# Halving the requests of attention's loads, and storing x from SyncE's queue instead of GpSimd's

## The chip, the cores and the metric

One Trainium2 chip, of which the program uses one core. The metric is the device time of one execution in microseconds (us), a median over runs. TensorE multiplies matrices, VectorE, ScalarE and GpSimd work on elements, SyncE issues DMAs and waits. All DMAs of the core, whichever engine issues them, are carried by the same 16 DMA engines.

## The reference

Two blocks in a row, all in float32. The first is causal sliding-window attention over 8 sequences of 576 rows, with 8 heads of 64 and a window of 64 keys. The second is a mixture of 8 experts, in which a row's expert is either its own best one or, where a local gate says so, that of the row before it.

```python
rel = pos[:, None] - pos[None, :]
mask = (rel >= 0) & (rel < window)
scores = np.where(mask, scale * np.matmul(q, k.transpose(0, 1, 3, 2)), -1e9)
attn = softmax(scores)                       # over keys
x = np.matmul(attn, v)                       # then (B, S, H*D): 4608 rows of 512

logits = x @ w_gate                          # 8 experts
local_gate = sigmoid(x @ w_local)
for b in range(B):
    for s in range(S):
        fresh_e = argmax(logits[b, s])
        e = fresh_e if s == 0 or local_gate[b, s] < 0.5 else prev_e
        prev_e = e
        h = np.maximum(x[b, s] @ w1[e], 0.0)           # 512 -> 1024
        out[b, s] = softmax(logits[b, s])[e] * (h @ w2[e])   # 1024 -> 512
```

## The kernel before

**Stages.** The 4608 rows are worked on in 9 groups of 512 (`sc` is 0 to 8). Attention takes each group in four units, one for each pair of heads (`hp` is 0 to 3), so it has 36 units. A unit is: `scores` (L385, 36 matmuls into two PSUM tiles `sp`), the exponential on ScalarE (L416) into a tile `p`, a mask on VectorE (L421) or a bias that TensorE adds beforehand, `values` (L431, 32 small matmuls into `xo`), and on VectorE the reciprocal of the row sums (L436) and the division that writes the unit's part of `x` (L441). Scores run two units ahead of values. When a group's four units are done its tile `x` (128 partitions by 4 chunks by 512 numbers, 1 MB) is stored to the DRAM tensor `xs`. Expert blocks then gather rows of `xs` by index (L1148), multiply them with `w1` and `w2` of their expert and scatter the result (L1361). The second stage starts when TensorE has done the last `values`, at about 134 us of 645.

**What attention loads.** For each group: `kq`, the keys and queries of the four head pairs (2 MB, into one tile `w` of a ring of four that the weights of the experts use later); `va`, the values with a column of ones (1 to 1.2 MB, three buffers), from which GpSimd (L361, L365) and ScalarE (L360, L363, L367) make a copy `vb` shifted by 64 rows; and, for groups 4 to 8, `vtt`, the values turned (1 MB, one buffer), from which TensorE computes the gates (`gates`, L317). The function `load` issues them on SyncE's queue, two groups ahead: `va` and the first half of `kq` after the first unit of group `sc` in program order, the second half of `kq` and `vtt` after its third. Attention's orders on TensorE, ScalarE and SyncE are written out by hand; VectorE and GpSimd are ordered by a scheduler.

**What SyncE waits for.** It executes its list in order, so a wait holds all that stands behind it. `va` of group `sc + 2` waits until TensorE has done the values of group `sc - 1`, whose buffer it takes. `vtt` waits for the gates of the group before. `until` (L239) is a DMA of four bytes that waits for an early or a late result, to hold the loads behind it back. Every DMA on the queue also takes one of eight completion semaphores in turn, and waits for the DMA that had it last. After attention's loads the queue carries the first experts' weights in 512 KB pieces (L1167), and `held` (L1471), a DMA of four bytes that waits for the first gathers, ahead of the weights of blocks 1 and 2.

**Where x is stored.** GpSimd issues one DMA for each group (L533), in its own order among the copies L361 and L365. The rows of `xs` are 528 numbers long, of which 512 are x, so that one row of one chunk is one run of 2 KB. `x` has two buffers: the first division of group `sc + 2` waits for the store of group `sc`. The first gathers wait for the stores of groups 0 to 3.

Of the kernel before, what the change touches and what calls it, by code (L numbers as in the profile page):

```python
# [19 lines left out]
P = 128  # L20
B, H, S, DH = 8, 8, 576, 64
D = H * DH
# [38 lines left out]
SC = 4 * P  # L61
# [7 lines left out]
GATED = range(4, NSC)  # L69
# [8 lines left out]
def row_of(t):  # L78

    return t + (t >= ZR)  # L80
# [87 lines left out]
def attention(ctx, tc, ring, kq, v3, v4, vt, vh, xs, lt, ok, wg, wg2, ident, rt, ex):  # L168
# [14 lines left out]
    nc = tc.nc  # L183
# [22 lines left out]
    kqs, qts, kts, vts, vas, vbs = {}, {}, {}, {}, {}, {}  # L206
# [4 lines left out]
    def space(name, sc):  # L211
        return kp.tile([P, 4, H, width(sc)], F32, name=name, bufs=2 if name == "vb" else 3)
# [6 lines left out]
    def load(sc, parts):  # L219
        for part in parts:  # L220
            if part == "turned":
                vts[sc] = tp.tile([P, HP, SC], F32, name="vtt")
                nc.sync.dma_start(out=vts[sc], in_=vt[GATED.index(sc)])
            elif isinstance(part, tuple):
                if sc not in vas:
                    vas[sc] = space("va", sc)
                src, h = v4[GATED.index(sc)] if sc in GATED else v3[sc], slice(*part)
                nc.sync.dma_start(out=vas[sc][:, :, h], in_=src[:, :, h])
            else:
                if sc not in kqs:  # L230
                    kqs[sc] = ring.tile([P, HP, 2, SC], F32, name="w")
                    kts[sc], qts[sc] = kqs[sc][:, :, 0], kqs[sc][:, :, 1]
                nc.sync.dma_start(out=kqs[sc][:, part], in_=kq[sc, :, part])

    late = cp.tile([1, 4], F32, name="late")

    def until(i, x):

        nc.sync.dma_start(out=late[:, i:i + 1], in_=x)  # L239

    pairs = slice(0, HP // 2), slice(HP // 2, HP)
    whole = (0, H)
    load(0, [slice(0, 1), slice(1, 2), (0, H // 2), pairs[1], (H // 2, H)])

    def warm(n):
# [39 lines left out]
    def build_bias():  # L285
        colf = columns()
        for c in range(2):
            for par in range(2):
                nc.vector.tensor_scalar(bias[:, c, :, par, :], colf[:, :KB // 2], rowf, LOW,
                                        Alu.is_lt if par == c else Alu.is_ge, Alu.mult)  # L290
        nc.vector.tensor_scalar(unit, colf[:, 0], rowf, None, Alu.is_equal)
        nc.vector.memset(never, LOW)
# [4 lines left out]
    def turn(sc, x, half):  # L297

        r = pair()
        for i in range(2):  # L300
            for c in range(4):
                nc.tensor.transpose(r[:, i, c * P:(c + 1) * P],
                                    x[:, c, 2 * half + i].rearrange("p j d -> p (j d)"), ident)
        o = pp.tile([P, 2, SC], F32, name="p")
        nc.scalar.copy(o, r)
        vts.setdefault(sc, []).append(o)
# [14 lines left out]
    def gates_ahead():  # L321

        r = bank()
        for hp in range(HP):
            nc.tensor.matmul(r[hp * GW:(hp + 1) * GW, :WIN], lhsT=wg2[:, hp, :], rhs=vhs[:, hp, :],
                             start=True, stop=True)
        nc.scalar.copy(ahead, r[:, :WIN])
# [7 lines left out]
    def logits(sc, gated):  # L335

        gt = back(gated).rearrange("p (c h g) -> p c g h", c=4, h=HP)[:, :, :E + 1]
        nc.vector.tensor_reduce(lt[:, 4 * sc:4 * sc + 4, :], gt, axis=AX.X, op=Alu.add)

    def spread(sc, gated):  # L340

        gt = back(gated).rearrange("p (c h g) -> p c h g", c=4, h=H)[:, :, :, :E + 1]
        g = slice(VX, VW)
        if sc == GATED[0]:
            nc.gpsimd.tensor_copy(vbs[sc][WIN:, 0, :, g], ahead_t[WIN:])
        nc.scalar.copy(vbs[sc][:WIN, :, :, g], gt[:WIN])
        nc.scalar.copy(vbs[sc][WIN:, 1:, :, g], gt[WIN:, :3])
        nc.scalar.copy(vas[sc][:, :, :, g], gt)

    def back_ahead():  # L350
        o = bank()[:WIN, :P]
        nc.tensor.transpose(o, ahead, ident)
        nc.scalar.copy(ahead_t[WIN:], o.rearrange("p (h g) -> p h g", h=H)[:, :, :E + 1])

    def shift(sc):

        va = vas[sc]
        vb = vbs[sc] = space("vb", sc)
        w = slice(width(sc - 1))
        nc.scalar.copy(vb[WIN:, 0, :, w], vas[sc - 1][WIN:, 3])  # L360
        nc.gpsimd.tensor_copy(vb[:WIN, :2], va[:WIN, :2])  # L361
        yield
        nc.scalar.copy(vb[WIN:, 1:3], va[WIN:, :2])  # L363
        yield
        nc.gpsimd.tensor_copy(vb[:WIN, 2:], va[:WIN, 2:])  # L365
        yield
        nc.scalar.copy(vb[WIN:, 3], va[WIN:, 2])  # L367

    def shift_first(half):

        va, h = vas[0], slice(4 * half, 4 * half + 4)
        if not half:
            vbs[0] = space("vb", 0)
            nc.gpsimd.memset(vbs[0][WIN:, 0], 0.0)
        nc.gpsimd.tensor_copy(vbs[0][:WIN, :, h], va[:WIN, :, h])
        nc.scalar.copy(vbs[0][WIN:, 1:, h], va[WIN:, :3, h])
# [82 lines left out]
    def step(free=True):  # L459
        nonlocal pause, side, trip  # L460
        pause -= HALF

        if side and pause <= 0.0 and (free or not trip):
            w, trip = next(side, (0.0, None))
            pause = max(pause, -HALF) + w
            if trip is None:
                side = ()
                if ex.jobs:
                    ex.rows(ex.jobs[0], -1)

    for i, (sc, hp) in enumerate(units):
        if hp == 0:
            x, g = wk.tile([P, 4, HP, 2, DH], F32, name="x"), None
            if sc in GATED:
                g = wk.tile([P, 4, HP, 2, E + 1], F32, name="g")

        if 1 < i < len(units) - LEAD:
            ps[units[i + LEAD]] = scores(*units[i + LEAD])
        if hp == (0 if sc else 3) and sc + 1 < NSC:
            moves = shift(sc + 1)  # L480
        for _ in range(2 if sc else 4):
            next(moves, None) if moves else None

        if hp == 3 and sc + 1 in GATED:
            spread(sc + 1, gated)
        elif (sc, hp) == (1, 3):
            gates_ahead()
        elif (sc, hp) == (2, 3):
            back_ahead()
        if hp == 3 and sc not in GATED:  # L490
            turn(sc, x, 0)
            old = x
        elif sc and sc - 1 not in GATED:
            if hp == 0:
                turn(sc - 1, old, 1)
            elif hp == 2:
                logits(sc - 1, turned)

        if side is None and 4 * sc >= C1 and hp >= 2:
            side = rt.first(bank)  # L500
        step(not (hp == 3 and sc + 1 in GATED))
        values(sc, hp, ps.pop((sc, hp)), x, g)
        if i < 2:
            ps[units[i + LEAD]] = scores(*units[i + LEAD])
        if i == 0:
            shift_first(1)
            until(1, allr[:1, 0, 0, 0, :1])
            load(2, [pairs[0], whole, pairs[1]])
            nc.sync.dma_start(out=vhs, in_=vh)
        if i == 2 * HP:  # L510
            with tc.issue_after(masked[-1].ins):
                rt.prepare()
                build_bias()
        if hp == 1 and sc and sc - 1 not in GATED:
            turned = gates(sc - 1)
        if hp == 2 and sc + 1 in GATED:
            gated = gates(sc + 1)
        if 0 < sc < NSC - 2 and hp in (0, 2):
            load(sc + 2, [pairs[1]] if hp else [whole, pairs[0]])
        if hp == 2 and sc + 2 in GATED:  # L520
            load(sc + 2, ["turned"])
        if (sc, hp) == (NSC - 3, 3):
            ex.jobs = [ex.weights({}, -1, ("w1",), lambda: until(2, allr[:1, sc, hp, 0, :1]))]
            if side == ():
                ex.rows(ex.jobs[0], -1)
        step(not (hp == 2 and sc + 1 in GATED))
        if (sc, hp) == (NSC - 2, 1):
            ex.weights(ex.jobs[0], -1, ("w2",), lambda: until(3, allr[:1, sc, hp, 0, :1]))
        if hp == HP - 1:
            if sc in GATED:  # L530
                nc.vector.tensor_reduce(lt[:, 4 * sc:4 * sc + 4, :], g.rearrange("p c h j e -> p c e (h j)"),
                                        axis=AX.X, op=Alu.add)
            nc.gpsimd.dma_start(out=xs[row_of(sc * SC):row_of(sc * SC) + SC, :D].rearrange("(c p) d -> p c d", p=P),  # L533
                                in_=x.rearrange("p c h j d -> p c (h j d)"))
    while side:
        step()

# [1030 lines left out]
```

## Time and profile before

| | |
|---|---|
| median of 3 runs (lowest, highest) | 646.91 us (645.65, 647.38) |
| the profiled execution | 646.97 us |
| its span, first to last instruction | 645.2 us |
| granted TensorE clock, mean | 0.997 |
| TensorE busy with matmuls in the span | 619.5 us (96%) |
| attention, 5 to 135 us | TensorE busy 116.0 of 130 us, DMA share 0.96, 363 GB/s |
| experts, 135 to 645.2 us | TensorE busy 501.1 of 510.2 us, DMA share 0.64, 231 GB/s |
| stores of x (L533), GpSimd | 9 of 1024 KB, 0.76 us each to issue |
| loads of kq | 17 of 1024 KB and 2 of 512 KB, issue to landing 10.2 us (median) |

The busy time of TensorE is modelled at the ends of its instructions, so its share says where it was supplied with work and not that it ran at its peak. The DMA share is the mean over the 16 DMA engines; it can come out a little over 1 in a short stretch, since a packet's time includes what it waited for on its way. "Idle before" in the timelines and waits is the time an engine stood still ahead of an instruction, with the event that ended it; "issue" means that the profile shows no event that it waited for.

### The profile page before, as it was taken

Reading aid. Unit: us, or ns where it says so; the run is one execution under the profiler, and the core shown is the slowest. Engines: PE = TensorE matmul, PEld = TensorE weight load, DVE = VectorE, ACT = ScalarE, POOL = GpSimd, SP = SyncE. Lnnn points to the kernel's source line nnn. Section 1 sums busy time; section 2 is a strip of 40 time slices with the busy share of each in tenths; the row PEclk is TensorE's granted clock in tenths of the full one; section 3 lists DMA queues with packets and bytes.
Section 4 is the critical chain, followed back from the end, with each engine's and each line's share of the span. In section 5 each row is a group of like instructions: output and inputs, shape, how many; then the busy total and the mean of one; then the engine's idle time right before and its main releaser. Section 6 shows DMA issues by size and latency. Waiting matters only on the chain. (4 is left out here: it accounts for less than half of the span.)

```text
span 645.2 us, 14856 instructions
## 1 busy us (share of the span) xinstructions
PE 619.5 (96%) x6319; PEld 535.8 (83%) x6319; DVE 386.7 (60%) x730; ACT 199.9 (31%) x364; POOL 130.0 (20%) x132
## 2 busy tenths in 40 slices
PE   8889998899999999999999999999999999999995
PEld 7777776785859999978998999887997998899995
DVE  6676588853874865273553683362917752876730
ACT  4766665611473122112120312021211221122120
POOL 5322112320003202111212220221312022101101
PEclk9999999999999999999999999999999999999998
DMA  8999999969736655686957655769768557945501
GB/s 331 416 349 344 379 359 368 344 241 356 210 146 233 242 199 197 209 314 244 398 193 274 229 226 217 259 232 366 258 244 302 186 196 255 354 157 221 216 17 38
DMA packets 29318, 166.43 MB, mean 258 GB/s; under 512 B 8451, under 2 KB 9497, under 8 KB 20026
## 3 DMA queue, kind: packets, MB, share of 16 engines
q1 hardware_dynamic: 20394, 135.54, 57.8%
q0 software_dynamic: 8848, 29.85, 11.9%
q8 instruction: 52, 0.85, 0.5%
q14 instruction: 24, 0.20, 0.1%
HBM read 146.18 MB, written 19.59 MB: 257 GB/s over the span
## 5 line engine op out<-in xcount | busy, mean ns | idle before, releaser
L1361 POOL DMA_INDIRECT out_dram<-y,idx x36 | 41.3, 1148 | 347.3 <-DVE y L1297 169.6
L1240 PE MATMUL hp<-xs,ws 128*128 128x128 f32 x672 | 79.6, 275 | 0.0
L1288 PE MATMUL hp<-ws,hs 128*128 128x256 f32 x336 | 77.6, 380 | 0.0
L1240 PEld LDWEIGHTS hp<-xs,ws 128*128 128x128 f32 x672 | 77.3, 192 | 0.0
L1288 PEld LDWEIGHTS hp<-ws,hs 128*128 128x128 f32 x336 | 63.5, 190 | 9.3 <-issue 0.8
L1379 PE MATMUL hp<-xt,w 128*64 128x64 f32 (+2 forms) x640 | 66.3, 276 | 1.0 <-issue 1.0
L1379 PEld LDWEIGHTS hp<-xt,w 128*128 128x128 f32 (+1 forms) x640 | 61.2, 170 | 5.9 <-issue 2.5
L1297 DVE SCALAR_TENSOR_TENSOR y<-hp,xg,kept 128x256 f32<-128x256 f32 x42 | 19.7, 481 | 71.4 <-issue 47.0
L1251 DVE TENSOR_TENSOR h<-hp,keep 128x512 f32<-128x512 f32 x42 | 28.6, 690 | 53.0 <-PE hp L1240 53.0
L1148 POOL DMA_INDIRECT xg<-xs,gx x40 | 48.2, 1205 | 44.3 <-issue 37.6
L1411 PE MATMUL yp<-w,h 128*128 128x512 f32 x128 | 56.6, 593 | 0.0
L1240 PEld LDWEIGHTS hp<-xt,w 128*128 128x128 f32 x448 | 53.2, 192 | 2.7 <-issue 1.3
L1240 PE MATMUL hp<-xt,w 128*128 128x128 f32 x448 | 54.7, 275 | 0.0
L1288 PE MATMUL hp<-w,h 128*128 128x256 f32 x224 | 53.6, 382 | 0.0
L431 PE MATMUL xo<-vb,p 128*64 128x74 f32 (+1 forms) x576 | 44.2, 228 | 6.8 <-issue 3.7
L416 ACT ACTIVATE p<-sp 128x512 f32<-128x512 f32 x72 | 39.2, 596 | 37.1 <-PE sp L385 33.9
L385 PEld LDWEIGHTS sp<-w 64*64 64x64 f32 x1296 | 37.9, 134 | 13.1 <-issue 9.7
L421 DVE TENSOR_TENSOR p<-p,mask 128x1024 f32<-128x1024 f32 x29 | 36.5, 1258 | 19.2 <-ACT p L416 18.9
L431 PEld LDWEIGHTS xo<-vb,p 128*64 128x64 f32 x576 | 38.4, 137 | 10.0 <-issue 5.2
L385 PE MATMUL sp<-w 64*64 64x128 f32 (+1 forms) x1296 | 43.3, 265 | 3.3 <-issue 2.4
L1288 PEld LDWEIGHTS hp<-w,h 128*128 128x128 f32 x224 | 41.3, 190 | 5.6 <-issue 0.4
L431 PE MATMUL xo<-va,p 128*64 128x74 f32 (+1 forms) x576 | 44.5, 228 | 1.5 <-issue 1.5
(280 smaller groups left out, 934.0 us busy)
## 6 DMA issues: line engine op xcount, KB each, us to landing
w<-in_w_dram SPq DMA_DIRECT2D x42, 2048.0 KB, 8.7
w<-in_kq_dram SPq DMA_DIRECT2D x17, 1024.0 KB, 10.2
w<-in_w_dram SPq DMA_DIRECT2D x24, 512.0 KB, 10.0
xs<-x POOLq DMA_DIRECT2D x9, 1024.0 KB
va<-in_v_dram SPq DMA_DIRECT2D x5, 1184.0 KB
vtt<-in_vt_dram SPq DMA_DIRECT2D x5, 1024.0 KB
va<-in_v_dram SPq DMA_DIRECT2D x3, 1040.0 KB, 10.2
va<-in_v_dram SPq DMA_DIRECT2D x2, 520.0 KB, 7.0
```

What stands on the lines that cost most here:

```text
L385: nc.tensor.matmul(sp[j][c * WIN:(c + 1) * WIN, a:b], lhsT=kt[h, hp, block * WIN:(block + 1) * WIN], rhs=qt[h, hp, a:b], start=not biased, ...
L416: nc.scalar.activation(p[:, j], sp[j], Act.Exp, scale=DH ** -0.5)
L421: masked.append(nc.vector.tensor_tensor(p, p, m.to_broadcast([P, 2, SC]), op=Alu.mult))
L431: nc.tensor.matmul(xo[par * WIN:(par + 1) * WIN, j, s * VW:s * VW + n], lhsT=p[:, j, b * WIN:(b + 1) * WIN], rhs=w[:, s, 2 * hp + j, :n], ...
L1148: self.nc.gpsimd.indirect_dma_start(out=x, out_offset=None, in_=self.xs[:rows, :], in_offset=bass.IndirectOffsetOnAxis(ap=gx[:, s:s + 1], ...
L1240: nc.tensor.matmul(out[:, m, :], lhsT=a[:, kk, m * P:(m + 1) * P], rhs=b[:, kk, :], start=start and m + kk == 0, stop=stop and (m, kk) == ...
L1251: nc.vector.tensor_tensor(o, x, y, op=add)
L1288: nc.tensor.matmul(out, lhsT=a[:, m, :], rhs=b[:, m, :], start=start and m == 0, stop=stop and m == FK // 2 - 1, skip_group_check=True)
L1297: nc.vector.scalar_tensor_tensor(y[i][:, j * w:(j + 1) * w], x, pw[i], y2, Alu.mult, Alu.add)
L1361: self.nc.gpsimd.indirect_dma_start(out=self.out[:, :], out_offset=bass.IndirectOffsetOnAxis(ap=st["idx"][:, s:s + 1], axis=0), in_=y, in_ ...
L1379: nc.tensor.matmul(hp[a, i, :], lhsT=st["w1"][:, kk, m * P:(m + 1) * P][:, a], rhs=st["xt"][:, kk, :n], start=(kk == 0), stop=(kk == DK - 1))
L1411: nc.tensor.matmul(yp, lhsT=st["h"][:, m, i * P:(i + 1) * P], rhs=st["w2"][:, m, :], start=(m == 0), stop=(m == FK - 1))
```

## The change

Attention's loads are requested in halves, and x is stored by SyncE:

- `vtt`: two DMAs of two head pairs each (512 KB) instead of one of 1 MB.
- `va`: where all eight heads were loaded at once, two DMAs of two chunks of 128 rows each (520 or 592 KB). The two half loads of group 0, four heads each, stay as they are.
- `kq`: one DMA for each head pair (512 KB) instead of one for two.
- `x`: two DMAs of 256 rows each (512 KB) on SyncE's queue, instead of one of 512 rows on GpSimd's. They stand at the same place of the program, after the last unit of the group, which is a place in SyncE's written order now: behind all loads issued in that group and ahead of those of the next.

```diff
             if part == "turned":
                 vts[sc] = tp.tile([P, HP, SC], F32, name="vtt")
-                nc.sync.dma_start(out=vts[sc], in_=vt[GATED.index(sc)])
+                for h in pairs:
+                    nc.sync.dma_start(out=vts[sc][:, h], in_=vt[GATED.index(sc), :, h])
             elif isinstance(part, tuple):
...
-                nc.sync.dma_start(out=vas[sc][:, :, h], in_=src[:, :, h])
+                for c in (slice(0, 2), slice(2, 4)) if h.stop - h.start == H else (slice(0, 4),):
+                    nc.sync.dma_start(out=vas[sc][:, c, h], in_=src[:, c, h])
             else:
...
-                nc.sync.dma_start(out=kqs[sc][:, part], in_=kq[sc, :, part])
+                for hp in range(part.start, part.stop):
+                    nc.sync.dma_start(out=kqs[sc][:, hp], in_=kq[sc, :, hp])
...
-            nc.gpsimd.dma_start(out=xs[row_of(sc * SC):row_of(sc * SC) + SC, :D].rearrange("(c p) d -> p c d", p=P),
-                                in_=x.rearrange("p c h j d -> p c (h j d)"))
+            for c in range(0, SC, SC // 2):
+                a = row_of(sc * SC) + c
+                nc.sync.dma_start(out=xs[a:a + SC // 2, :D].rearrange("(c p) d -> p c d", p=P),
+                                  in_=x[:, c // P:(c + SC // 2) // P].rearrange("p c h j d -> p c (h j d)"))
```

`pairs` is the two halves of the four head pairs, `HP` is 4, `H` 8, `P` 128 and `SC` 512. The order of matmuls on TensorE is the same in both kernels; 26 more of them carry a wait, because the halves have a semaphore each.

## The prediction

> **What bounds the kernel.** I read the page first, then the stages.
>
> ```profile
> span 645.2 us, 14856 instructions
> PE 619.5 (96%) x6319; PEld 535.8 (83%) x6319; DVE 386.7 (60%) x730; ACT 199.9 (31%) x364; POOL 130.0 (20%) x132
> ...
> PE   8889998899999999999999999999999999999995
> ...
> q8 instruction: 52, 0.85, 0.5%
> ```
>
> TensorE (PE) is the bound at 96%, and apart from the tail its digits fall under 9 only in the first eight slices, which are attention. The last line is the engines' own fetch of instructions: 52 packets of 16 KB, against TensorE's 12,812 records, one packet for some 250. The table of stages says how full the DMA engines are meanwhile:
>
> ```profile
> 5.00:135.00 130.00, 116.00 (x2735) 95.67 (x2735) 96.70 (x239) 79.50 (x135) 34.06 (x41) 1.00 0.96 363
> 135.00:645.20 510.20, 501.09 (x3576) 437.68 (x3574) 289.48 (x490) 119.07 (x228) 91.98 (x79) 1.00 0.64 231
> 75.00:80.00 5.00, 4.31 (x86) 2.83 (x85) 2.80 (x10) 1.87 (x4) 0.00 (x0) 1.00 1.01 412
> 155.00:160.00 5.00, 5.00 (x16) 2.56 (x15) 2.64 (x13) 0.69 (x1) 1.04 (x1) 1.00 1.03 419
> ```
>
> Columns: stretch, its length, busy time of PE, PEld, DVE, ACT and POOL, granted clock, DMA share, GB/s. Attention leaves TensorE idle for 14 of 130 us with the DMA engines 96% busy; after 135 us it is idle for 9 of 510. The change touches attention alone, so what it is worth lies in those 14 us. Who ends them, from TensorE's waits up to 135 us:
>
> ```profile
> PE xo L431 <- issue: 5.2, 6, 1.8
> ...
> PE sp L385 <- issue: 2.4, 4, 1.1
> PE xo L431 <- DVE x L441: 1.6, 2, 1.2
> PE xo L431 <- ACT p L305: 1.5, 3, 0.8
> ...
> PE xo L302 <- issue: 0.5, 1, 0.5
> ```
>
> No load ends a wait. Eleven gaps, 5.2 + 2.4 + 0.5 = 8.1 us, are ended by nothing that the profile knows, and they cut groups of matmuls in two, as in the timeline of TensorE:
>
> ```profile
> 127.44 0.23 PE L431 MATMUL xo<-vb,p 128*64 128x74 f32 x1
> 129.43 0.22 PE L431 MATMUL xo<-vb,p 128*64 128x74 f32 x1 [1.75 <-issue]
> ```
>
> I numbered TensorE's records and set them against the q8 packets. Eight of the gaps stand at records 705, 961, 1217, 1473, 1985, 3009, 4033 and 5057, each 449 above a multiple of 256, and each ends 1.2 to 1.5 us after a q8 packet has ended (the gap shown ends at 129.43, the packet at 128.10). They are late instruction fetches. From a block's end to the next packet's start it is 1.3 us where the load queue had just run dry (51.91 to 53.20; 82.22 to 83.45), and 3.0 to 4.5 us in nearly all blocks where DMA was full. A block lasts 4.4 to 6.2 us, so a fetch that takes 4.4 + 1.0 + 1.4 = 6.8 us from block's end to first matmul is late, and one that takes 1.3 + 1.0 + 1.4 = 3.7 is not.
>
> **The change, part by part.**
>
> *Halves in place of 1 MB.* No bytes are added. The 3 us that a fetch loses to a full queue are about ten of the 8 KB packets that kq and vtt are made of (309 ns each). With 4 KB packets (159 ns in the trace) ten cost 1.6 us, 1.5 less; if it is bytes and not packets that stand ahead, nothing changes. For packets: at 9.80 us, among packets mostly of 1040 bytes, the delay was only 1.7 us; at 111.98, among 64-byte ones, 1.9, both with DMA full. For bytes: at 116.33 and 123.25, with 4 KB packets of the weights but GpSimd's store beside them, it was 4.5 and 3.8. I take packets, two rows that differ by themselves against two that a second queue disturbs, and 1.5 us earlier per fetch. The eleven gaps are 0.51, 0.43, 0.65, 1.09, 0.24, 0.28, 0.69, 1.02, 0.27, 1.18 and 1.75. The first (20.48) frees nothing, since ScalarE is busy without a break from 19.84 to 27.83; nor does the eighth (100.10), since TensorE next waits for VectorE's L441 until 103.07. The other nine hold 6.6; cut by at most 1.5 each, 6.3. Behind a gap the next wait is the chain through ScalarE and VectorE, so I count three quarters: **-4.7 us** (bounds 0 and -6.6).
>
> The Trainium skill speaks for this ("DMA: Bandwidth & Descriptors", Queues, rings and completion order): a DMA engine turns from one queue to the next only after a whole packet of typically 9 to 17 descriptors. By it a fetch would wait for one load's share of an engine, eight packets: 2.5 us now and 1.3 us in halves, and the sum would be 0.2 us less.
>
> *Cost of more requests.* The row against any loss of rate is the pair of stretches above: 1 MB pieces at 75 to 80 us moved 412 GB/s, 512 KB weight pieces at 155 to 160 us moved 419. Zero. SyncE issues some 50 DMAs more at 0.33 to 0.45 us, 20 us spread over 130 in which it mostly waits. With eight semaphores, only eight DMAs can be under way, so the queue ahead shrinks to seven halves, 3.6 MB or 8.7 us at 412 GB/s: still a cover.
>
> The skill has a rule against the change (same page, Bandwidth): batch DMAs to at least 1 MiB for 75% of peak. With its fixed 2.0 us plus bytes at 436 GB/s, and nothing overlapped, each MB would cost 2 us more, an estimate of 70 us over attention's 35 MB of loads; the 419 GB/s here contradict it for queued DMAs.
>
> *x on SyncE's queue.* GpSimd loses nine issues of 0.76 us, in front of nothing that is late: 0. Its stores interleaved with the loads; now their 1 MB (2.6 us) stands in line. Worse is the wait: SyncE stops at each store until VectorE's last L441 of the group, with the next va, kq and vtt behind it. In groups 0 to 4 that is about 1.0 us after the values end, which is what lets va go now. In group 5 it is not:
>
> ```profile
> 100.55 1.49 DVE L951 TENSOR_TENSOR rowh<-io,lo 128x1280 bf16<-128x1280 f32 x1
> ...
> 102.34 0.68 DVE L441 TENSOR_TENSOR x<-xo,allr 128x512 f32<-128x512 f32 x1
> ```
>
> ```profile
> 97.00 0.33 SPq L228 DMA_DIRECT2D va<-in_v_dram  x1
> 97.38 1.73 SPq L233 DMA_DIRECT2D w<-in_kq_dram  x2
> 108.59 0.33 SPq L223 DMA_DIRECT2D vtt<-in_vt_dram  x1
> ```
>
> VectorE has 8 us of the router in front of that division, which ends at 103.02, so va of group 8, issued at 97.00 now, goes at about 103.9. Adding up the queue from 103.0 (first byte 1.0, store 2.6, va 2.9, kq 5.1, vtt 2.6, and 0.5 from a landing to its reader): va is there at 110.0, needed at 111.6 by L361; kq at 112.6 to 115.1, needed from 116.3; vtt at 117.7, needed at 118.5 (L317). All hold, by 0.8 us at worst. The stores of the last three groups move behind the weights of block 0: x of group 6, landed at 119.6 now, goes behind the small rows of L893 (1.6) and four 512 KB pieces (5.1) and lands at 117.2 + 1.6 + 5.1 + 2.6 = 126.5, or 127.8 with the first gathers between; the division of group 8 that takes its buffer starts at 127.8. Cost **+0.3** (bounds 0 and +6). In the other groups va and kq have 6 to 15 us in hand, and the 2.6 us of the store fit. The stores of groups 7 and 8 are asked for when GpSimd asked, 125.2 and 135; blocks 1 and 2 still wait for their gathers (143.25).
>
> *More waits on TensorE.* 26 more matmuls carry one. A wait of its own took 51 ns on the weight-load queue (L431's row of semaphore events): 0 to 1.3, taken as **+0.2**, most of it under running matmuls.
>
> *GpSimd's store out of the fetch's way* is inside the first term; with one load queue fewer to share with, it can only shorten the delay.
>
> Sum: -4.7 + 0.3 + 0.2 = -4.2. The profiled execution took 646.97 us, 1.8 outside its span and 0.06 above the median: 646.97 - 4.2 = **642.8 us**.
>
> **Rivals.**
>
> 1. *The fetch waits for bytes.* The halves change nothing and the cover of the loads is enough: -1 to +0.8, about 647. For: the 3.8 to 4.5 us beside 4 KB packets; fetches between 16 KB packets of the experts, whose delay looks like 3 to 4.5 us and not twice that. Against: the two short delays among small packets.
> 2. *Slower: the store in SyncE's order starves attention's end.* Place: group 5's division, with group 8's loads behind it. It decides if the queue runs 0.8 us later than added up, or TensorE reaches L317 of group 8 that much sooner, which the first term itself brings about; moved group by group, the store's own wait moves with TensorE, but VectorE's 8 us do not shrink. Price: the loads are 6.9 us later at issue plus 2.6 for the store, 9.5; vtt has 118.5 - 115.7 = 2.8 in hand; at most 6.7 without the first term, some 3 as a middle: 650, up to 653.6. For: DMA is dry at 101 to 104 in that case, at 96% share. Against: the margins above, thin but none negative.
> 3. *The change does not do what it says*: no. In the instruction lists each 128x2048 load is two of 128x1024, and TensorE's and VectorE's orders are the same.
>
> **How the numbers follow.** The forecast (fetches earlier, -2 to -8) has 0.60; rival 1 0.18; rival 2 0.22. 0.3% is 1.9 us, about what a measurement of this kernel can tell from none. Faster by more: the forecast's 0.60 and 0.02 of rival 1. Within: 0.15. Slower: 0.23. The low end is the full 6.6 and 1.3 more from waits that shrink with them, 639.0; 0.08 lies beyond. The high end, 649.5, leaves out the worse half of rival 2. The forecast alone would be 639 to 645.
>
> **What would show it.** Right: TensorE's "issue" waits up to 135 us fall from 8.1 to under 4, q8 packets start within 3 us of a block's end, and the last L431 moves from 133.8 to about 129.6, with the 510 us behind it unchanged. Wrong by rival 1: the eleven gaps stand where they were. Wrong by rival 2: TensorE waits for DMA vtt or va, or VectorE's L441 for the store, after 105 us. A loss of rate would show as under 400 GB/s in attention's full stretches.

## The result, and the profile after

The kernel after took 658.1 us (median of four runs, 656.67 to 658.89), the kernel before 646.43 beside it: a ratio of 1.0165, 95% interval 1.0142 to 1.0188. Forecast was 642.8. The profiled execution took 658.72 us, 1.7 of it outside the span. The page of the kernel after:

```profile
span 657.0 us, 14910 instructions
...
PE 621.3 (95%) x6319; PEld 536.9 (82%) x6319; DVE 387.0 (59%) x730; ACT 199.7 (30%) x364; POOL 122.9 (19%) x123
...
PE   8889998779999999999999999999999999999991
...
PEclk9999999989999999999999999999999999999996
```

TensorE does the same 6319 matmuls. Two places are new: the eighth and ninth slices (115 to 148 us), where the granted clock dips as well, and the last slice, nearly empty where it had a 5 before. Its two stages, columns as in the prediction (stretch, length, busy time of PE, PEld, DVE, ACT and POOL, granted clock, DMA share, GB/s):

```profile
5.00:135.00 130.00, 112.90 (x2661) 93.00 (x2662) 93.00 (x229) 78.14 (x133) 27.55 (x33) 0.98 0.95 350
135.00:657.00 522.00, 505.98 (x3652) 441.54 (x3650) 293.48 (x500) 120.28 (x230) 91.48 (x78) 0.99 0.63 230
```

Since the order of the matmuls is the same, each can be set against its twin. The kernel after is 2.1 us late at 11.8 us, 1.1 us early at 115, 5.8 late at 138 us, and then keeps these 5.8 through the experts to within 0.1 until about 546 us, where the profiled execution of before loses 1.7 us between matmuls of L1379. The last matmul ends 3.9 us later (642.27 against 638.41), and from there to the end of the span it takes 14.7 us instead of 6.8. So 3.9 + 7.9 = 11.8, the difference of the spans.

The 1.7 us at 546 belong to neither kernel: nine of the study's eighteen profiles have them, at 545 to 555 us, and which ones goes by the group of runs. The first profile of before and the second of after have them, the second of before and the first of after do not. Like against like, the last matmul of the kernel after comes 4.6 us (without) or 5.0 us (with) later, and its span is 12.6 or 12.8 us longer.

**The end.** Nothing computes or moves there. GpSimd closes the program with two instructions of its own, an INC_SWDGE_SEM and then a DRAIN. The lines give operation, count, duration in ns as minimum, median and maximum, and first and last start. After:

```profile
L1569 POOLq DRAIN  x3: 46/103/7012, 649.1 to 656.7; - x3
...
L136 POOLq INC_SWDGE_SEM  x1: 1900/1900/1900, 647.2 to 647.2; - x1
```

Before:

```profile
L1564 POOLq DRAIN  x3: 50/103/1050, 643.3 to 644.9; - x3
...
L136 POOLq INC_SWDGE_SEM  x1: 440/440/440, 642.8 to 642.8; - x1
```

Together 8.91 us instead of 1.49; all engines meet behind it. That is 7.4 of the 7.9.

**The end of attention.** TensorE's waits up to 135 us, after:

```profile
PE xo L434 <- DVE x L444: 4.9, 3, 4.0
PE xo L434 <- issue: 4.5, 3, 2.1
...
PE sp L388 <- issue: 1.4, 1, 1.4
```

The wait of 4.0 us for VectorE's division (L444, L441 before) is new. VectorE's timeline says what the division waits for, and TensorE's that it waits for the division:

```profile
127.53 0.23 DVE L442 TENSOR_TENSOR g<-xo,allr 128x72 f32<-128x72 f32 x1
133.92 0.69 DVE L444 TENSOR_TENSOR x<-xo,allr 128x512 f32<-128x512 f32 x1 [6.16 <-DMA xs<-x]
```

```profile
134.76 0.36 PE L434 MATMUL xo<-vb,p 128*64 128x74 f32 x1 [4.02 <-DVE x L444]
```

It is the first division of group 8, and it waits 6.16 us for the store of x of group 6 to leave the buffer. SyncE's timeline shows where that store stood:

```profile
109.47 7.66 SPq L898 DMA_DIRECT2D xs<-ptw  x2
...
118.91 2.47 SPq L1172 DMA_DIRECT2D w<-in_w_dram  x4
121.49 1.10 SPq L538 DMA_DIRECT2D xs<-x  x2
...
129.88 3.00 SPq L538 DMA_DIRECT2D xs<-x  x2
```

Asked for at 121.49 and 121.92, behind the small rows (L898) and four pieces of w1, its halves landed at 132.48 and 133.83 (the last of the 16 completion events of each). Before, GpSimd's store, asked for at 114.08, had landed by 123.9.

**The clock.** Four stretches of the kernel after, cut where the granted clock changes (columns as above):

```profile
127.61:131.02 3.41, 1.20 (x30) 1.04 (x29) 0.15 (x1) 0.70 (x2) 0.00 (x0) 1.00 1.03 399
131.02:134.43 3.41, 0.00 (x0) 0.00 (x0) 0.51 (x1) 0.00 (x0) 0.00 (x0) 0.50 1.04 420
134.43:137.85 3.42, 3.09 (x37) 2.97 (x38) 3.04 (x8) 0.00 (x0) 0.00 (x0) 0.50 1.02 401
137.85:141.26 3.41, 3.41 (x45) 2.98 (x45) 1.80 (x6) 1.07 (x2) 0.00 (x0) 1.00 0.50 177
```

Two stretches with 2.2 and 3.4 us of idle time, each followed by one at half the clock (a halved stretch, below). The first matmuls behind the stall, between 134.8 and 137.6 us, take 1.4 us more than their twins. Before, the emptiest stretch of this kind had 1.93 us of matmuls, and the clock behind it stayed whole:

```profile
125.74:129.15 3.41, 1.93 (x59) 1.69 (x56) 2.82 (x6) 1.61 (x4) 0.54 (x1) 1.00 1.03 383
129.15:132.57 3.42, 3.14 (x69) 2.89 (x68) 2.51 (x7) 0.31 (x1) 0.00 (x0) 1.00 1.00 367
```

The Trainium skill says this of TensorE ("TensorE: Matmul & The Clock Gate", Part 1): the clock is halved after an idle window of 3.413 us, and the windows run freely and do not start with the kernel. The stretches of 3.41, 6.83 and 10.24 us at clock 0.50 in the runs here agree in length. In one point they differ: the window need not be idle, for the first one above still had 1.20 us of matmuls. Free-running windows also fit the 2.1 us at the start: the clock rose at 6.27 us in the kernel before, at 11.55 in this execution and at 8.03 in a second one of the same kernel, which was only 0.45 us behind at 11.8.

### The profile page after: what moved, and what is told of

It reads as the page before. It is cut to its first block, busy times and chain, and to the rows that moved or that the text cites. A ratio compares the mean times of both kernels' runs of the same rounds, so it can differ in the third digit from the quotient of the medians.

```text
span 657.0 us, 14910 instructions
## 1 busy us (share of the span) xinstructions
PE 621.3 (95%) x6319; PEld 536.9 (82%) x6319; DVE 387.0 (59%) x730; ACT 199.7 (30%) x364; POOL 122.9 (19%) x123
## 5 line engine op out<-in xcount | busy, mean ns | idle before, releaser
L388 PEld LDWEIGHTS sp<-w 64*64 64x64 f32 x1296 | 38.9, 138 | 11.8 <-issue 5.8
```

What stands on the lines that cost most here:

```text
L388: nc.tensor.matmul(sp[j][c * WIN:(c + 1) * WIN, a:b], lhsT=kt[h, hp, block * WIN:(block + 1) * WIN], rhs=qt[h, hp, a:b], start=not biased, ...
```

## The experiments

Theory A: both losses come from the stores of x, through GpSimd's DRAIN and the buffer of group 6. Theory B: they come from the halves. Each result is given with its ratio to the runs of the kernel before on the same chip, whose medians were 647.15, 648.39, 646.16 and 647.07 us in the four groups of runs.

**One part of the change at a time.** The first keeps the halves and GpSimd's store:

```
-            for c in range(0, SC, SC // 2):
-                ...
-                nc.sync.dma_start(out=xs[a:a + SC // 2, :D]...)
+            nc.gpsimd.dma_start(out=xs[row_of(sc * SC):row_of(sc * SC) + SC, :D]..., in_=x...)
```

> Edit: the loads in halves as in the kernel after, x stored by GpSimd in one piece as in the kernel before. Theory A (both losses come with the stores of x: 4.0 us of TensorE waiting for L444 near 131 us and 1.4 of a halved clock behind it, and 6.0 to 8.0 in GpSimd's last DRAIN, 7.01 us instead of 1.05): neither is here, so 645 to 648 us, the DRAIN near 1 us, no wait for L444 over 2 us after 125 us. Theory B (the halves themselves cost, by the granted clock that rose 5 us later at the start, or by more requests): 648.5 or more, with the losses of the trace after in part. If the first term of the prediction had been right, 642 to 643.

Measured: 650.01 us, 1.0052 (1.0017 to 1.0087); in the profile a span of 644.6, a DRAIN of 1.05 us, no wait for the store. Neither loss is there. But this profile is of one of the fastest of ten executions (646.34 to 655.23), and the median lies where theory B had it: something of 0.2 to 0.9% is there.

The second is the opposite, the kernel before with only the store changed:

```
-            nc.gpsimd.dma_start(out=xs[row_of(sc * SC):row_of(sc * SC) + SC, :D]..., in_=x...)
+            for c in range(0, SC, SC // 2):
+                ...
+                nc.sync.dma_start(out=xs[a:a + SC // 2, :D]..., in_=...)
```

> Edit: x stored from SyncE's queue in two pieces as in the kernel after, the loads in 1 MB pieces as in the kernel before. Theory A (both losses come with the stores): 655 to 660 us, a wait of TensorE for L444 of about 4 us near 131 us, GpSimd's last DRAIN about 7 us. Theory B (the halves cost): 647 to 650. If the halves gain in the middle of attention what the trace after suggests (about 2 us between 11 and 105 us), this is about 2 us above the kernel after, 659 to 661.

Measured: 654.67 us, 1.0119 (1.0085 to 1.0153). The DRAIN takes 7.01 + 1.90 us, 7.4 us more than in the kernel before, which is nearly all of the 7.5 between the medians. The stall is not here. VectorE's division of group 8 hardly waited for the store, and no matmul waited for it (TensorE's wait of 2.1 us for L441 stands at 102 us, at the division of group 5):

```profile
132.01 0.69 DVE L441 TENSOR_TENSOR x<-xo,allr 128x512 f32<-128x512 f32 x1 [0.20 <-DMA xs<-x]
```

The profiled execution is the slowest of five (659.12; the others 653.42 to 655.69): its last matmul comes 4.0 us late, with three halved stretches of 3.4 us. So theory A holds for the DRAIN, and theory B falls for it. The stall, though, stands only in profiles that have both the halves and the stores behind w1 (five of them); with 1 MB loads and the stores behind w1 there is this one profile, without it, and whether it needs the halves is not shown.

**The stall.** In the next the two stores of group 6 stand ahead of the first request for w1:

```
+        if hp == HP - 1 and sc == NSC - 3:
+            ... (the block of the two stores)
         if (sc, hp) == (NSC - 3, 3):
             ex.jobs = [ex.weights({}, -1, ("w1",), ...
...
-        if hp == HP - 1:
+        if hp == HP - 1 and sc != NSC - 3:
```

> Edit: the kernel after, but in group 6 the two stores of x stand ahead of the first request for w1 in SyncE's order. Theory A (the stall of 4.0 us at the division of group 8 is the store of group 6 behind w1 in the queue, and the halved clock behind it follows from that stall): the store lands before 128 us, the wait for L444 and the clock's dip are gone, 652 to 654.5 us, with the DRAIN still near 7 us. If the dip of the clock has another cause: 653.5 to 655. If the stall is not the store's: 657 to 659.

Measured: 653.98 us, 1.0123 (1.0089 to 1.0156). The stores landed at 121.44 and 122.79, the profile has no halved stretch, and the last matmul ends at 635.22, 7 us sooner than in the kernel after. That flatters it, since the profiled execution is the fastest of four (651.54; the others 653.60 to 654.59): by the medians' ratios it is 0.42%, some 2.7 us. Its waits from 100 to 142 us (a kernel of 649.8 us):

```profile
PE xo L434 <- DVE x L444: 2.2, 2, 1.9
PE sp L388 <- issue: 1.4, 1, 1.4
```

The wait of 4.0 us has gone (the 1.9 stands at 102 us, at the division of group 5 behind the router's work on VectorE) and the DRAIN of 7.01 has stayed: two separate losses.

Giving the last three stores back to GpSimd takes the store out of SyncE's order too:

```
+            if sc >= NSC - 3:
+                nc.gpsimd.dma_start(out=xs[row_of(sc * SC):...], in_=x...)
+                continue
             for c in range(0, SC, SC // 2):
```

> Edit: the kernel after, but x of groups 6, 7 and 8 is stored by GpSimd as in the kernel before (groups 0 to 5 from SyncE's queue in two pieces). Theory A: no store stands behind w1, so no wait for L444 of 4 us near 131 us and no halved clock behind it: the last matmul about 635 to 637, as with the store ahead of w1. GpSimd's DRAIN and INC_SWDGE_SEM, by theory D (0.1 us for each of 88 software DMAs, if three stores of 512 pieces do not yet reach the number from which they are cleared): 9.2 us in sum, 652 to 655; if they reach it, 2 to 6 in sum, 646 to 650.

Measured: 658.25 us, 1.0170 (1.0131 to 1.0208), where 652 to 655 was expected. The wait for the division is gone, as expected, but the last matmul came at 641.98, some 1.8 us of it from the loss at about 546 us, which this profile has. From 112 us on TensorE waits for

```profile
PE sp L388 <- issue: 3.1, 4, 1.5
PE r L320 <- DMA vtt<-in_vt_dram: 1.5, 1, 1.5
```

GpSimd's store now runs beside vtt of group 8, whose last packet ends at 123.03 (119.39 in the kernel after): the prediction's second rival, in a kernel that it was not written for. The sum at the end is 7.26 + 1.96 = 9.22, as theory D had it.

A second profile of the kernel after:

> The kernel after, a second profiled execution. Fixed places should come again: the DRAIN of 7.0 us, the wait for L444 at the division of group 8 (3 to 5 us) with at least one halved stretch of 3.4 us behind it. Chance places need not: the clock's rise at 11.6 us instead of 6.3 (2 us). Time 656 to 659.

Measured: 659.76 us, DRAIN 7.01. The division of group 8 waits again:

```profile
133.00 0.69 DVE L444 TENSOR_TENSOR x<-xo,allr 128x512 f32<-128x512 f32 x1 [4.67 <-DMA xs<-x]
```

TensorE's wait for it is 4.1 us, with one halved stretch of 3.4 behind it. The time is above the 656 to 659 expected; this profile has the loss at about 546 us, the first did not.

**GpSimd's DRAIN.** The kernel after with nine more GpSimd DMAs of 256 pieces:

```
+            nc.gpsimd.dma_start(out=dump[sc * P:(sc + 1) * P].rearrange("p (c o) -> p c o", c=2)[:, :, :4],
+                                in_=x[:, 0:2, HP - 1, 1, 0:4])
```

> Edit: the kernel after, and behind each group's stores of x one more DMA from GpSimd, 256 descriptors of 16 bytes from x into rows that nothing reads (36 KB in all nine). Theory A1 (GpSimd's last DRAIN depends on how many software DMAs or descriptors it has issued; nine more of 256 descriptors restore the count of the kernel before): the DRAIN goes from 7.0 to about 1 us and the time to 650 to 652. Theory A2 (the DRAIN is long for another reason, such as a store from SyncE's queue, or by chance): 657 to 660 and a DRAIN near 7.

Measured: 660.87 us, 1.0216 (1.0182 to 1.0250), and the DRAIN grew:

```profile
L1573 POOLq DRAIN  x3: 46/103/7747, 653.0 to 661.3; - x3
```

With the 2.08 us ahead of it that is 9.83, 0.92 more for nine DMAs, 0.102 us each; 8.91 for the 85 that GpSimd issues in the kernel after (software DMAs, below) is 0.105 each, and the 88 of the run with three stores given back fit with 9.22. In these three it is a price per software DMA. Theory A1 in its plain form (the count) falls: 94 of them took 1.49 in the kernel before. The next gives the nine as many pieces as a store of x has, and little data (with the stores of group 6 ahead of w1):

```
+            if i >= NSC and len(jobs[0].setdefault("more", [])) < NSC:
+                ...
+                tc.nc.gpsimd.dma_start(out=to[:, :, :4], in_=self.ident[:, :16].rearrange("p (c d) -> p c d", c=4))
```

> Edit: the kernel with the store of group 6 ahead of w1 (651.5 in its profiled run, 654.0 median), and among the experts, nine times, one more GpSimd DMA of 512 pieces of 16 bytes, as many pieces as a store of x has, but 8 KB and not 1 MB. It leaves TensorE alone. GpSimd's DRAIN and the INC_SWDGE_SEM before it took 7.01 + 1.90 us with 85 software DMAs, 7.75 + 2.08 with 94 of which nine had 256 pieces, 1.05 + 0.44 with 94 of which nine were whole stores of x. Theory D (0.1 us at the end for every software DMA that GpSimd has not yet cleared away, and clearing away begins once a fixed number of pieces is exceeded): about 1.5 in sum, 7.4 us less than the parent, 644 to 647 us. Theory E (bytes or packets moved count): 9.8 in sum as with 256 pieces, 654 to 656. Theory F (the store from SyncE's queue makes the DRAIN long): 8.9 to 9.8, the same time.

```profile
L1583 POOLq DRAIN  x3: 46/103/1050, 650.6 to 652.5; - x3
```

1.05 + 0.44, with the stores still on SyncE's queue and 8 KB instead of 1 MB each: theory D, neither E nor F. The time, 651.49 us, 1.0053 (1.0028 to 1.0079), fell less than 7.4: reading a constant, the nine were issued in attention and not among the experts, as GpSimd's timeline shows:

```profile
15.21 6.00 POOL L1512 DMA_DIRECT2D dump<-ident  x8
```

The fetch at 20.6 us then came after 6.3 us instead of 4.4, and the last matmul ended at 645.08, with three halved stretches and the loss at about 546 us. The same on the kernel after, and its expectation:

> Edit: the kernel after, unchanged up to the experts, and there nine more GpSimd DMAs of 512 pieces of 16 bytes. It takes away the long DRAIN alone. Theory A with D (the 11.7 us between the two medians are about 7.4 at GpSimd's last DRAIN and INC_SWDGE_SEM and the rest at the end of attention): DRAIN 1.05 us, the stall for L444 near 131 us still there in the profile (3 to 5 us, with a halved clock after it), 649 to 652.5 us, about 0.5% above the kernel before. If the time at the end is not the DRAIN's: 656 to 659.

Measured: 656.24 us, 1.0154 (1.0111 to 1.0197), where 649 to 652.5 was expected. The DRAIN is 1.05, TensorE's wait for the division of group 8 is 1.9 us with 10.2 us of halved clock from 133.2, and TensorE's longest gap without a cause is most likely the price of the nine early DMAs (fetch delay 7.3 us):

```profile
31.35 0.92 PE L389 MATMUL sp<-w 64*64 64x128 f32 x12 [3.92 <-issue]
```

With nine whole megabytes from w1 in their place, which can only be issued late (in_=jobs[i]["w1"][:, :, :D]):

> Edit: as the run before, but the nine extra GpSimd DMAs are 1 MB each, 512 pieces of 2 KB, as large as the stores of x were (from w1 of the running block into rows that nothing reads, among the experts where the DMA engines are busy 64%). Theories D and E: DRAIN and INC_SWDGE_SEM about 1.5 us in sum as in the kernel before, the span some 7 us under the parent's 649.8, unless the extra 9 MB get in the way of weights. Theory F (the store from SyncE's queue makes it long): 9 to 10 in sum.

Measured in one run: span 648.3 us, DRAIN 1.05 + 0.44. That is 1.5 us less than the parent, where some 7 was expected: TensorE ran 4.4 us later, 1.7 of it from a late rise of the clock at the start (11.85 us) and 1.8 from the loss at about 546 us, which the parent's profile does not have.

Small and late (in_=jobs[i]["w1"][:, :, :4]), on the kernel after:

> Edit: the kernel after, and among the experts nine more GpSimd DMAs of 512 pieces of 16 bytes, each of which reads the running block's w1 and so cannot be issued before it has landed. The earlier nine read a constant and were issued at 15 to 22 us, in attention, where they put a gap of 4 us into TensorE's work; these cannot. Theory D: DRAIN 1.05 us, nothing else moved, 7.4 us less than the kernel after: 649.5 to 652. If the long DRAIN hides something that would end as late anyway: 656 to 659.

Measured: 653.16 us, 1.0083 (1.0044 to 1.0122), 0.82% or about 5 us less than the kernel after. The sum at the end fell by 7.42; 1.2 came back ahead of it (from the last matmul to INC_SWDGE_SEM 6.1 us instead of 4.9).

**Both mended.** The stores of group 6 ahead of w1 and the nine late small DMAs:

> Edit: the kernel after, the stores of group 6 ahead of w1, and the nine late small DMAs: both losses mended, the halves and SyncE's stores kept. By the parent's 654.0 and 7.4 for the DRAIN: 645.5 to 648, the same as the kernel before within 0.3%. If the halves and the stores were worth what the prediction gave them: 642 to 644. If something besides the two losses costs: 649 and more.

Measured: 648.51 us, 1.0010 (0.9971 to 1.0049): the kernel before. On the same chip it is 4.7 us below the run that has the DRAIN mended alone. Not all of that need be the stall. In that run's own profile TensorE's wait for the division of group 8 was 1.7 us, without a halved stretch behind it, and 3.3 us of the difference between the two profiles stood already at 115 us, ahead of the stores that were moved:

```profile
134.74 0.69 DVE L445 TENSOR_TENSOR x<-xo,allr 128x512 f32<-128x512 f32 x1 [2.31 <-DMA xs<-x]
```

The price of the stall can be read directly, from TensorE's 2661st matmul, just ahead of it, to the 2791st at about 150 us: 20.1 and 20.3 us in the two profiles of the kernel after, 21.5 and 19.5 in the two with nine more GpSimd DMAs in attention, 16.4 with the DRAIN mended alone, against 15.2 and 15.3 with the stores ahead of w1. So it cost 4.2 to 6.2 us in four of five executions and 1.1 in the fifth.

And the same with loads of 1 MB:

> Edit: loads in 1 MB pieces as in the kernel before, x stored from SyncE's queue in two pieces, those of group 6 ahead of w1, and the nine late small DMAs. The halves alone measured 0.5% (0.2 to 0.9) above the kernel before. If that is theirs, this is 2 to 3 us under the run with both mended: 643 to 646. If the halves cost nothing and those ten runs were chance: the same as that run within 1.5 us.

Measured: 649.30 us, 1.0031 (0.9987 to 1.0076), 0.8 us above the halves, where 2 to 3 below was expected if they cost 0.5%.

**The halves.** Quarters show whether the size of a packet matters to the fetch:

```
-                for hp in range(part.start, part.stop):
-                    nc.sync.dma_start(out=kqs[sc][:, hp], in_=kq[sc, :, hp])
+                for hp in range(part.start, part.stop):
+                    for i in range(2):
+                        nc.sync.dma_start(out=kqs[sc][:, hp, i], in_=kq[sc, :, hp, i])
```

(va and vtt likewise.)

> Edit: loads in quarters (256 KB, 2 KB packets for kq and vtt), x stored by GpSimd as in the kernel before. In full stretches of attention a fetch of instructions started 3.0 to 4.4 us after its block's end with 8 KB packets and 2.9 to 4.2 with 4 KB packets. If bytes stand ahead of it: still 3 to 4.4, TensorE's waits without a cause up to 135 us stay at 5 to 8 us. If packets down to some size count: under 2.5, waits under 4 us. Time 644 to 652 by either, more if the number of requests on SyncE's queue (about 100 more than before) begins to cost.

Measured: 654.57 us in one run, above the 644 to 652 expected, with two halved stretches in attention. TensorE's waits without a cause up to 135 us are 8.6 us. From a block's end to its q8 packet, over the blocks 1 to 17, the median is 3.51 us with these 2 KB packets. With 8 KB it is 3.40 and 3.61 in two profiles of the kernel before, with 4 KB (halves alone) 3.55, 3.49 and 3.36. The delay does not follow the size of the packets.

Three further profiles, two of the halves alone and one of the kernel before:

> The halves without the stores, a second profiled execution of the same program: ten runs of it had a median 0.5% above the kernel before and ranged from 646.3 to 655.2 us, and the one that has a profile was 646.5. Theory G (the halves cost by chance meetings: a gap of TensorE of over about 1.6 us within one of the clock's free-running windows of 3.41 us halves the clock in the next, 1.7 us each, and which gaps do so differs from run to run): one to three halved stretches of 3.4 or 6.8 us between 10 and 140 us, 1.7 us of time for each 3.4, the rest of the trace as in the first. Theory H (the halves cost at a fixed place, such as a load that lands late): the same wait for a load or a division of over 1 us in both profiles that the kernel before does not have.

> The same program as in the run before, a third profiled execution; the same expectations.

> The kernel before, a second profiled execution. Theory G: its gaps are the same ones, the longest windows stay just under 1.6 us of idle time in most places, no or one halved stretch in attention; the gap of about 1.7 us at 546 us in its first profile, which no other kernel's profile has, is gone; time 644 to 650. GpSimd's last DRAIN 1.05 us again.

Measured: 647.21, 649.57 and 646.14 us. The third execution of the halves has the late start of the clock (11.72 us, 2.1 us); the two have no halved stretch in attention, the first execution has one. In the second profile of before, the gap at 546 us is gone. Theory H has one small place: TensorE's wait for the division of group 5, at 102 to 106 us, was 1.2 and 0.5 us in the two profiles before and is 2.3, 1.5 and 2.0 with halves, so about 1 us of what TensorE might save ahead of it goes there to VectorE. That makes a gain vanish and no loss. Theory G is not shown either: the executions of 650 to 655 us have no trace.

**Both parts together.** Set side by side, the profiles show a gain that no median does. From TensorE's 94th matmul, at about 10 us, to its 2352nd, at about 115, the kernel before takes 105.4 and 106.7 us and the halves alone 107.2 (with one halved stretch), 106.1 and 106.4. With halves and SyncE's stores it is 102.3 and 103.0 in the kernel after and 103.1, 103.2 and 103.9 in three of its variants (the other variants have a halved stretch there or the early DMAs, but for the one with three stores given back to GpSimd, at 105.9). So some 3 us are won by 115 us in these five. What brings them was not tested apart: stores alone have halved stretches in both their profiles (105.8 and 107.4). With both losses mended, the last matmul is 1.0 us earlier than in the first profile of before, and the end behind it takes 8.5 us instead of 6.8, for which no run shows a cause.

## Why the prediction was wrong

**Halves in place of 1 MB: -4.7, measured none by themselves.** The step that failed is "I take packets". The delay is the same with packets of 8, 4 and 2 KB (medians 3.4 to 3.6 us), so TensorE's waits without a cause stay: 8.1 and 9.1 us in two profiles before, 5.3, 8.7 and 7.4 in three with halves alone. The two rows that were read as "packets" do not show that a fetch waits for a number of them: 500 packets of 1323 bytes in 1.67 us were 0.66 MB at 395 GB/s, which is no emptier a queue than the 1.5 MB in 4.41 us, 350 GB/s, among 8 KB packets. Short delays stand at full rate in every size (2.1 us at 425 GB/s in the kernel before, 1.8 at 394 with quarters), and what sets them stays open. The skill's rule, which the prediction weighed beside this step ("DMA: Bandwidth & Descriptors", Queues, rings and completion order: an engine turns to the next queue after a whole packet), would by the prediction's estimate have had 2.5 us fall to 1.3 with halves; 3.4 to 3.6 in every size does not agree. Rival 1 had the unchanged delay right; that the fetch waits for bytes is not shown either. With SyncE's stores beside the halves, the gain of some 3 us up to 115 us is in the direction of this term, and the kernel after does not keep it.

**Cost of more requests: 0, about right.** 413 GB/s in the full stretch from 132 to 134 us. Whether the halves cost anything by themselves stays open: 0.2 to 0.9% in one comparison, -0.8 us in the other.

**x on SyncE's queue: +0.3 (0 to +6), measured 2.7 and 4.7 in two pairs of medians.** Place, buffer and reader were named, and the price lay within the bounds, but for one execution at 6.2; the middle was mis-sized. The division was to start at 127.8 and started at 133.92. (GpSimd's store of group 6 had landed by 123.9 in the kernel before, not at 119.6: its first completion event is at 120.45.) The sum let the rows start when vtt had landed at 117.2, and everything behind run at full rate. vtt landed at 119.39; the second L898 held SyncE for 5.58 us, to 117.1, so the first w1 piece was issued only at 118.91; from 118 to 126 us the DMA engines moved 104 to 295 GB/s; and the store took 6.5 us from its first packet to the end of its last (126.78 to 133.31) instead of 2.6, since it did not have the engines to itself: of the 2.66 MB that they moved in that time 1.05 were the store, 1.05 pieces of weights and 0.54 the first gathers. And a stall of 4 us brings its halved clock, 1.4 us, which the sum did not have.

**"GpSimd loses nine issues of 0.76 us, in front of nothing that is late: 0": measured +7.4.** This is the largest error, and not one of size: nothing in the prediction dealt with the end of the kernel. The step that failed is the 0: it weighed only what GpSimd's issues stand in front of. The runs showed 8.91 us of INC_SWDGE_SEM and DRAIN in place of 1.49, and 1.49 again once GpSimd had nine other DMAs of 512 pieces. The row stood in the profile of before, a DRAIN of 1.05 us behind which every engine waits, but not that its length hangs on what GpSimd has issued. The honest step would have been to list what else depends on GpSimd's DMAs, and to bound it.

**"The 510 us behind it unchanged"** held to 0.1 us up to about 546 us. The loss of 1.7 us there comes and goes with the group of runs in either kernel, so the expectation of the second profile of before, that no other kernel's profile has it, was wrong.

**Rival 2** had the sign and the wrong place: va, kq and vtt of group 8 held. Its mechanism appeared where GpSimd's store ran beside vtt.

The account by the ratios: DRAIN 0.82% (the kernel after 1.0165, with it mended 1.0083), stall 0.73% (1.0083 to 1.0010; by the other pair, 1.0165 to 1.0123, only 0.42%), the rest 0.1% with an interval of 0.4 to either side. The first two are known to about half a per cent, an estimate from the intervals of the ratios that they are taken from. The halves and SyncE's stores together are worth nothing that the medians show, and no version beat the kernel before.

## What to carry to other kernels

Moving a DMA to another engine's queue changes more than who issues it: ask what the old queue does at the end with the DMAs it no longer has, and read the last rows of the profile, not only the bottleneck's. A store whose buffer is taken again soon must not be asked for behind prefetches that nobody needs yet. Two rows with small packets and short delays are no evidence for a count of packets: short delays stood among large packets too. Change the size of the packets alone and compare the delay over many blocks.

## What the hardware showed that was not expected

- GpSimd's closing INC_SWDGE_SEM and DRAIN took 8.91 us with 85 software DMAs, 9.22 with 88 and 9.83 with 94, about 0.10 us each; but 1.49 with 94 of which nine had 512 pieces, whether of 2 KB or of 16 bytes, early or late. It looks as if GpSimd clears its list away once a number of pieces is passed (94 with nine of 256 pieces did not pass it, nor 88 with three of 512); no run here shows that number or when the clearing is done.
- Among the stretches of 3.41 us at full clock in all eighteen profiles, every one with 2.0 us or more of TensorE's idle time had the clock halved in the next (such as the 2.2 us from 127.61 above); none with under 1.3 us had; between them both occurred (1.32 halved; 1.90 not, nor the 1.5 us from 125.74 in the kernel before). Behind stretches that were halved themselves, 0.9 to 1.0 us of it came before one more halved stretch in three profiles. As the stretches do not start with the kernel, the same gap costs in one execution and not in the next: the wait at the division of group 5 was 2.3 us with a halved stretch behind it in the first execution of the halves, and 2.0 without one in the third.
- Nine DMAs of 8 KB from GpSimd, issued at 15 to 22 us into a full load queue, came with one instruction fetch of 6.3 and 7.3 us instead of 4.4. The same fetch took 6.1 with loads in quarters and without these DMAs, so they need not be the only cause.
